# Unread products on TensorE: ahead of the first loads, in the attention's first batch, and between the gate's logits

## The chip, the cores and the metric

The kernel runs on one core of a Trainium2 chip. Its engines are TensorE (PE; its weight loads are shown apart as PEld), VectorE (DVE), ScalarE (ACT), GpSimd (POOL) and SyncE (SP), whose queue issues the DMAs. Each runs its own queue in order and waits for the others on semaphores. The metric is the device time of one execution in microseconds (us), as the median of several runs. [...]

## The reference

Attention over 2 batches, 8 heads, 576 positions and 64 dimensions, once on positions averaged in fours and once in a band of width 4, summed; then 8 dense experts that a Sinkhorn iteration weighs; then one MLP with softplus.

```python
    q_d = q.reshape(B, H, Sd, factor, D).mean(axis=3)        # k_d, v_d alike
    out_up = np.repeat(sm_attn(q_d, k_d, v_d), factor, axis=2)
    mask = np.abs(pos[:, None] - pos[None, :]) < factor
    scores = np.where(mask, scale * np.matmul(q, k.transpose(0, 1, 3, 2)), -1000000000.0)
    ...
    x = (out_up + out_local).transpose(0, 2, 1, 3).reshape(B * S, H * D)     # 1152 x 512

    logits = x @ w_gate                                       # 512 x 8
    P = np.exp(logits - logits.max())
    for _ in range(8):
        P /= P.sum(1, keepdims=True) + 1e-09
        P /= P.sum(0, keepdims=True) + 1e-09
        P *= N / E
    for e in range(E):
        out += P[:, e:e + 1] * (np.maximum(x @ w1[e], 0.0) @ w2[e])

    h = out @ w_in                                            # 512 x 2048
    return (np.maximum(h, 0.0) + np.log1p(np.exp(-np.abs(h)))) @ w_out
```

## The kernel before

The attention works in eight units, four of the first batch and then four of the second; a unit is two heads. A unit has four blocks: `c`, the coarse scores of all 144 averaged positions, and 0, 1, 2, the band in three thirds. `load` (L492) fetches a unit's q and k (`qk`, one buffer only, so that the next unit's load can begin only when the last transposes of this one have read it) and its values in two forms (`vw`, `vd`). `setup(g)` (L514, g = 0, 1, 2) transposes a third of q and k on PE (tile `tb`, L523); VectorE and ScalarE make `kT`, `fine`, `flat` and `qkd` of it. `scores` (L551) multiplies them into a PSUM bank `sc`: L557 for the coarse block, L564 (mask) and L570 for a third of the band. VectorE and ScalarE do the softmax and leave the weights in `ex`. `turn` (L588) transposes `ex` (tile `tp`, L596 coarse, L605 band), ScalarE copies it to `et`, and `values` (L609) multiplies it by the values (tile `pv`, L616 coarse, L627 band). In the first batch the banks of `sc` rotate over three (`m0` to `m2`), those of `tb` and `tp` over four (`at`), and `pv` has one (`y`).

The main loop (L1028) walks through the stream of 32 blocks with `turn` two and `values` three blocks behind `scores`, and sets a unit's `setup` beside the last two blocks of the one before. Beside the first batch it fetches the first expert's weights (`fetch_first`, `fetch_second`: a load to `raw`, casts on ScalarE to `w1h` and `w2h`, remainders and sums on GpSimd). The vectors x, and the sums and differences of them that a seven-product scheme needs, are split into two parts, `xh` and `xl` (`operands`, L419). From the second batch on, `beside` (L987) mixes in the first expert's products, `m` (L831) and `yps` (L919).

After the attention the second half of the operands is made, and `gates` (L672) computes the logits: `lt` (L683), a product with 16 columns of `wgs`, is copied to `lts` by ScalarE, and nine small products `lg` (L690; each with 16 rows, 128 columns of `lts` as weights and 8 columns of `fold`) write the logits of 128 positions each into one bank, of which only the first 72 columns are read. Two rounds of `m` products follow (`lead`).

Up to here the order of the instructions on each engine is set when the program is built, by a scheduler that runs a model of the engines and puts each instruction where it becomes ready; it may move an instruction ahead of others on its engine as long as the data allow it. From the loop after that on (L1098), the order is written out by a planner with fixed durations.

## Time and profile before

| | us |
|---|---|
| median of 3 runs | 1078.72 (1078.42 to 1078.95) |
| profiled execution, its own time | 1076.35 |
| its span, first to last instruction | 1074.3 |
| PE busy in the span | 1047.9 (98%) |
| DVE, ACT, POOL busy | 698.1, 568.5, 556.9 |
| longest in the chain that ended last | `yps` L919 40%, `m` L831 36% |

The profile is one execution, read by the hardware profiler; times in its rows are us from the span's start. Busy time of PE counts an instruction as long as it is in the pipe, so neighbours overlap: what a product costs in a stream is the distance between starts.

### The profile page before, as it was taken

How to read it: one execution, taken by the hardware profiler on the slowest of the kernel's cores; microseconds unless marked ns; L12 is line 12 of the kernel's file. 1: busy time of each engine (PE TensorE's matmuls, PEld its weight loads, DVE VectorE, ACT ScalarE, POOL GpSimd, SP SyncE). 2: the span in 40 equal slices, each digit the busy share in tenths (PEclk: the TensorE clock that was granted, in tenths of full speed). 3: DMA queues.
4: the chain of work that ended last, by engine and by line, in shares of the span. 5: the costliest groups of instructions: out<-in, count | busy, mean ns of one | idle time of the engine just before them, and what ended most of it. 6: DMA issues, size and time to landing. Idle time of an engine off the chain costs nothing.

```text
span 1074.3 us, 17657 instructions
## 1 busy us (share of the span) xinstructions
PE 1047.9 (98%) x6385; PEld 932.8 (87%) x6385; DVE 698.1 (65%) x1430; ACT 568.5 (53%) x1475; POOL 556.9 (52%) x575
## 2 busy tenths in 40 slices
PE   6989999999999999999999999999999999999998
PEld 5768888888989999898999989898988999789987
DVE  4797655776566566665656566565664778776765
ACT  4788634444444444454444444444454667676663
POOL 4567514477575565555556566664575412232221
PEclk9899989999999999999999999999999999999999
DMA  7553301122433334333333333343334473253112
GB/s 169 115 141 86 92 1 40 60 87 86 145 97 94 113 93 133 98 118 118 114 117 93 94 102 105 105 117 118 118 98 138 145 294 140 108 228 136 69 40 89
DMA packets 133495, 119.69 MB, mean 111 GB/s; under 512 B 35744, under 2 KB 111776, under 8 KB 133408
## 3 DMA queue, kind: packets, MB, share of 16 engines
q1 hardware_dynamic: 133408, 118.56, 35.6%
q8 instruction: 50, 0.82, 0.3%
q14 instruction: 37, 0.30, 0.1%
HBM read 93.11 MB, written 25.43 MB: 110 GB/s over the span
## 4 chain that ended last, share of the span: by engine, by line
PE 82%; DVE 9%; ACT 4%; POOL 1%; issue 1%; SPq 1%; DMA 1%; ACTq 0%
PE yps L919 40%; PE m L831 36%; DVE ab L798 1%; POOL ab L795 1%; DVE ab L791 1%; ACT one L793 1%; PE sc L570 1%; DVE xl L441 1%; DVE one L789 1%; PE tb L523 1%; PE tp L605 1%; DMA qk<-in_k 1%; PE pv L627 1%; SPq L499 1%; DVE c L850 1%
## 5 line engine op out<-in xcount | busy, mean ns | idle before, releaser
L831 PE MATMUL m<-xh,w1h 128*128 128x320 f32 (+1 forms) x1120 | 334.2, 299 | 3.6 <-DVE hl L770 1.6
L831 PE MATMUL m<-xh,w1l 128*128 128x320 f32 (+1 forms) x1120 | 332.8, 297 | 0.0
L831 PE MATMUL m<-xl,w1h 128*128 128x320 f32 (+1 forms) x1120 | 332.6, 297 | 0.0
L831 PEld LDWEIGHTS m<-xh,w1h 128*128 128x128 f32 x1120 | 212.6, 190 | 21.1 <-ACT t L843 3.5
L831 PEld LDWEIGHTS m<-xl,w1h 128*128 128x128 f32 x1120 | 212.7, 190 | 13.0 <-DVE xl L441 0.2
L831 PEld LDWEIGHTS m<-xh,w1l 128*128 128x128 f32 x1120 | 212.5, 190 | 0.3 <-issue 0.2
L919 PE MATMUL yps<-w2h,hh 128*128 128x512 f32 x502 | 198.9, 396 | 2.2 <-ACT hh L800 2.2
L919 PE MATMUL yps<-w2l,hh 128*128 128x512 f32 x502 | 198.2, 395 | 0.0
L919 PE MATMUL yps<-w2h,hl 128*128 128x512 f32 x502 | 196.0, 390 | 0.0
L919 PE MATMUL yps<-w2h,h 128*128 128x512 f32 x436 | 153.0, 392 | 0.1
L850 DVE TENSOR_TENSOR c<-m,t 128x256 f32<-128x256 f32 (+1 forms) x160 | 72.8, 455 | 113.8 <-PE m L831 67.5
L295 POOL TENSOR_TENSOR w1l<-sums,w1h 128x512 fp32r<-128x512 f32 x72 | 99.6, 1395 | 86.9 <-ACT w1h L293 75.3
L316 POOL TENSOR_TENSOR w2l<-raw,w2h 128x512 fp32r<-128x512 f32 x72 | 98.7, 1390 | 59.6 <-ACT w2h L314 56.1
L795 POOL TENSOR_TENSOR ab<-one,ab 128x320 f32<-128x320 f32 (+1 forms) x64 | 54.6, 855 | 143.6 <-ACT one L793 143.6
L768 ACT ACTIVATE hh<-c 128x256 fp32r<-128x256 f32 (+1 forms) x138 | 60.7, 445 | 128.5 <-DVE c L850 128.5
L949 DVE SCALAR_TENSOR_TENSOR acc<-yps,pr,acc 128x512 f32<-128x512 f32 x117 | 87.3, 746 | 55.2 <-PE yps L919 54.5
L770 DVE SCALAR_TENSOR_TENSOR hl<-c,hh 128x256 fp32r<-128x256 f32 (+1 forms) x138 | 94.7, 690 | 32.1 <-ACT hh L768 30.4
L919 PEld LDWEIGHTS yps<-w2h,hl 128*128 128x128 f32 x502 | 94.4, 188 | 21.7 <-DVE hl L802 0.2
L919 PEld LDWEIGHTS yps<-w2h,hh 128*128 128x128 f32 x502 | 94.7, 189 | 15.2 <-ACT hh L800 2.6
L843 ACT COPY t<-m 128x256 f32<-128x256 f32 (+1 forms) x160 | 63.4, 398 | 79.6 <-PE m L831 79.3
L919 PEld LDWEIGHTS yps<-w2l,hh 128*128 128x128 f32 x502 | 94.7, 189 | 10.9
L919 PEld LDWEIGHTS yps<-w2h,h 128*128 128x128 f32 x436 | 82.0, 188 | 15.2 <-ACT h L800 0.3
(136 smaller groups left out, 1653.6 us busy)
## 6 DMA issues: line engine op xcount, KB each, us to landing
raw<-in_moe_w SPq DMA_DIRECT2D x72, 256.0 KB
raw<-in_moe_w SPq DMA_DIRECT2D x36, 512.0 KB
w1h<-s_in SPq DMA_DIRECT2D x10, 896.0 KB
w1l<-s_in SPq DMA_DIRECT2D x10, 896.0 KB
raw<-in_moe_w_in SPq DMA_DIRECT2D x32, 256.0 KB
raw<-in_moe_w_out SPq DMA_DIRECT2D x16, 512.0 KB
w2l<-s_out SPq DMA_DIRECT2D x10, 512.0 KB
w2h<-s_out SPq DMA_DIRECT2D x10, 512.0 KB
```

The lines of the kernel that those rows point to most:

```text
L295: behind(chain, nc.gpsimd.tensor_tensor(lo[:, part], sums, hi[:, part].bitcast(F32), op=ALU.subtract))
L316: behind(chain, nc.gpsimd.tensor_tensor(lo[:, i], raw[:, i], hi[:, i].bitcast(F32), op=ALU.subtract))
L441: nc.vector.tensor_tensor(xl[s][:, i, kk], src, xh[s][:, i, kk].bitcast(F32), op=ALU.subtract)
L499: nc.sync.dma_start(qk[w * QT : (w + 1) * QT, cut, hh], src[b, h0 + hh].rearrange("(t p) d -> p t d", p=QT)[:, cut],)
L768: nc.scalar.activation(hh, c, AF.Relu)
L770: nc.vector.scalar_tensor_tensor(out=hl, in0=c, scalar=0.0, in1=hh.bitcast(F32), op0=ALU.max, op1=ALU.subtract)
L795: nc.gpsimd.tensor_tensor(ab, one, ab, op=ALU.subtract)
L831: nc.tensor.matmul(b[:, :h], x[:, i, kk, :], y[s][:, i, kk, :], start=(not more and n == 0), stop=(n == 5), skip_group_check=more,)
L843: nc.scalar.copy(t, b[:, :h])
L850: nc.vector.tensor_tensor(c, b[:, :h], t, op=ALU.add)
L919: nc.tensor.matmul(y, a[:, f, tok], b[:, f, :], start=(start and m == 0), stop=(stop and m == 5))
L949: nc.vector.scalar_tensor_tensor(out=acc[t], in0=y, scalar=pr[:, t, e : e + 1], in1=acc[t], op0=ALU.mult, op1=ALU.add,)
```

## The change

A helper `stir` puts unread products of the bf16 identity with itself, four times side by side (512 columns), into a bank that is overwritten afterwards. Eight stand ahead of the first `setup`. In unit 0 one stands ahead of the scores of each of the four blocks, two ahead of the coarse transposes and one ahead of each band block's; in units 1 to 3 one ahead of the coarse transposes and one ahead of each band block's. That makes 29. In `gates` an unread product of 256 columns, of `xh` with itself, follows every second logit product, four in all; it writes columns of the bank that nobody reads.

```diff
+    def stir(out, times):
+        for _ in range(times):
+            nc.tensor.matmul(
+                out.rearrange("p (a c) -> p a c", c=P), identb, identb.unsqueeze(1).to_broadcast([P, 4, P]),
+                start=True, stop=True,
+            )
...
         def __init__(self, n, b, u):
-            self.b, self.u = b, u
+            self.n, self.b, self.u = n, b, u
...
             sc = self.bank("sc", 0)
+            stir(sc, 1 if self.n == 0 else 0)
             if blk == "c":
...
                     tp = self.bank("tp", 1)
+                    stir(tp, 1 if self.n == 0 or self.n < 4 and c == 0 else 0)
                     for i in range(NB):
...
                 tp = self.bank("tp", 1)
+                stir(tp, 1 if self.n < 4 else 0)
                 for i in range(NB):
...
                 nc.tensor.matmul(lg[:, t * E : (t + 1) * E], lts[:, o : o + P], fold, start=True, stop=True)
+                if t % 2:
+                    busy = xh[s][:, 4, 0]
+                    nc.tensor.matmul(lg[:, 2 * P : 4 * P], busy[:, :P], busy[:, : 2 * P], start=True, stop=True)
...
     stream = [(x, blk) for x in units for blk in blocks]
+    stir(units[0].bank("pv", 2), 8)
     for g in range(NB):
         units[0].setup(g)
```

The scheduler sets the order up to the planner's loop anew. On PE, at the third unit's transposes of q and k (`tb`) and the second unit's coarse transposes (`tp`), where pass 2 of the prediction begins, there stood:

```order
L570 MATMUL sc<-kT,fine_150 128x72 x3
L523 MATMUL tb<-ident,qk 128x128 x6
L627 MATMUL pv<-et,vw 64x64 x12
L596 MATMUL tp<-ident,ex 72x96 x6
L564 LDWEIGHTS identb
L564 MATMUL sc<-mask,identb 128x216
L570 MATMUL sc<-kT,fine_151 128x72 x3
```

and now stands:

```order
L578 MATMUL sc<-kT,fine_150 128x72 x3
L637 MATMUL pv<-et,vw 64x64 x6
L530 MATMUL tb<-ident,qk 128x128 x6
L481 LDWEIGHTS identb
L481 MATMUL tp<-identb 128x512
L637 MATMUL pv<-et,vw 64x64 x6
L605 MATMUL tp<-ident,ex 72x96 x6
L572 LDWEIGHTS identb
L572 MATMUL sc<-mask,identb 128x216
L578 MATMUL sc<-kT,fine_151 128x72 x3
```

One unread product has come between, and half of the value products has moved ahead of the transposes of q and k.

On PE at the logits (`lg`), between products of the next round (`m`), there stood:

```order
L831 MATMUL m_2155<-xh_2027,w1l 128x320
L690 MATMUL lg<-fold,lts 128x8 x6
L831 MATMUL m_2127<-xh_2027,w1h 128x320
L831 MATMUL m_2127<-xl_2028,w1h 128x320
L831 MATMUL m_2127<-xh_2027,w1l 128x320
```

and now stands:

```order
L844 MATMUL m_2189<-xh_2057,w1l 128x320
L700 MATMUL lg<-fold,lts 128x8 x2
L703 MATMUL lg<-xh_103 128x256
L700 MATMUL lg<-fold,lts 128x8 x2
L703 MATMUL lg<-xh_103 128x256
L700 MATMUL lg<-fold,lts 128x8 x2
L703 MATMUL lg<-xh_2057 128x256
L844 MATMUL m_2161<-xh_2057,w1h 128x320
```

The unread products stand after each pair of logit products. The last three logit products, six `m` products further on before, now come after three `m` products, with the fourth unread product among them.

On SP, where the second unit's loads are issued (its `vw` first at the ends and then in the middle, its `qk`, its `vd`), there stood:

```order
L505 DMA vw<-in_v 72x2x64 x2
L499 DMA qk<-in_q 64x9x64 x2
L499 DMA qk<-in_k 64x9x64 x2
L509 DMA vw<-in_v 72x7x64 x2
L512 DMA vd<-in_v 72x2x256 x2
```

and now stands:

```order
L512 DMA vw<-in_v 72x2x64 x2
L516 DMA vw<-in_v 72x7x64 x2
L506 DMA qk<-in_q 64x9x64 x2
L506 DMA qk<-in_k 64x9x64 x2
L519 DMA vd<-in_v 72x2x256 x2
```

The larger part of `vw` has moved ahead of `qk`.

## Rows read from the trace of the kernel before

**Rows 1.** The page: granted TensorE clock in 40 slices of the span, in tenths.

```profile
PEclk9899989999999999999999999999999999999999
```

**Rows 2.** Stretches: width, busy us (instructions) of PE, PEld, DVE, ACT, POOL; PEclk; DMA.

```profile
12.00:30.00 18.00, 15.44 (x81) 12.45 (x81) 8.35 (x28) 8.97 (x42) 6.24 (x11) 1.00 0.73 169
30.00:42.00 12.00, 9.96 (x114) 8.11 (x112) 9.75 (x34) 10.26 (x51) 1.64 (x4) 1.00 0.49 103
42.00:54.00 12.00, 11.58 (x67) 9.55 (x67) 8.71 (x31) 9.58 (x38) 11.25 (x13) 0.57 0.69 147
54.00:70.00 16.00, 11.96 (x135) 9.83 (x134) 15.68 (x42) 12.20 (x47) 12.33 (x14) 1.00 0.54 144
...
80.00:140.00 60.00, 60.00 (x523) 51.42 (x523) 39.30 (x111) 39.91 (x148) 35.13 (x37) 1.00 0.32 82
...
152.00:160.00 8.00, 8.00 (x34) 7.65 (x35) 2.21 (x7) 1.78 (x6) 0.00 (x0) 0.57 0.01 2
```

**Rows 3.** Timeline of PE, first units: start, duration, operation, idle time before and its releaser.

```profile
6.72 2.15 PE L523 MATMUL tb<-ident,qk 128*128 128x128 f32 x9 [6.72 <-DMA vd<-in_v]
...
14.55 1.54 PE L523 MATMUL tb<-ident,qk 128*128 128x128 f32 x6 [0.65 <-DMA qk<-in_k]
18.00 1.15 PE L596 MATMUL tp<-ident,ex 96*72 96x96 f32 x6 [1.91 <-DVE ex L585]
...
24.57 1.43 PE L570 MATMUL sc<-kT,fine 128*128 128x72 f32 x6
...
29.86 0.82 PE L523 MATMUL tb<-ident,qk 128*128 128x128 f32 x6
```

**Rows 4.** Timeline of PE, the next pass.

```profile
32.64 0.69 PE L596 MATMUL tp<-ident,ex 96*72 96x96 f32 x6 [0.25 <-DVE ex L585]
...
33.90 0.49 PE L523 MATMUL tb<-ident,qk 128*128 128x128 f32 x3
...
38.70 0.80 PE L570 MATMUL sc<-kT,fine 128*128 128x72 f32 x6
40.18 0.85 PE L523 MATMUL tb<-ident,qk 128*128 128x128 f32 x6 [0.68 <-DMA qk<-in_k]
```

**Rows 5.** Timeline of PE, the pass after that, and the fifth unit's first transposes.

```profile
42.99 1.17 PE L596 MATMUL tp<-ident,ex 96*72 96x96 f32 x6 [0.25 <-DVE ex L585]
...
44.14 1.43 PE L570 MATMUL sc<-kT,fine 128*128 128x72 f32 x6
...
53.16 0.86 PE L570 MATMUL sc<-kT,fine 128*128 128x72 f32 x6
...
54.45 0.88 PE L523 MATMUL tb<-ident,qk 128*128 128x128 f32 x6
```

**Rows 6.** Timeline of VectorE: the identity in bf16.

```profile
1.74 0.21 DVE L459 CAST identb<-ident 128x128 bf16<-128x128 f32 x1
```

**Rows 7.** The chain that ended last: start, us on the chain, what.

```profile
36.44 3.61 DMA qk<-in_k
...
101.08 2.76 PE yps L919 x12
...
181.83 1.75 PE m L831 x12
```

**Rows 8.** Timeline of PE, the logits and the products after them.

```profile
150.41 1.50 PE L690 MATMUL lg<-fold,lts 16*128 16x8 f32 x12 [0.47 <-ACT lts L687]
...
153.40 1.45 PE L690 MATMUL lg<-fold,lts 16*128 16x8 f32 x6
...
158.15 0.47 PE L831 MATMUL m<-xh,w1h 128*128 128x320 f32 x1
158.41 0.47 PE L831 MATMUL m<-xl,w1h 128*128 128x320 f32 x1
```

**Rows 9.** Waits of PE from 140 to 200 us: us in total, times, longest.

```profile
PE m L831 <- DVE hl L770: 1.6, 2, 1.1
```

**Rows 10.** Timeline of VectorE behind the logits.

```profile
158.38 0.49 DVE L850 TENSOR_TENSOR c<-m,t 128x320 f32<-128x320 f32 x1 [2.73 <-PE m L831]
```

## The prediction

> **What bounds the kernel now.** I read the slices of the page first: the granted clock of TensorE is below 9 tenths in two places of the span's first sixth and nowhere after it [rows 1]. So only the first 160 us can be worth anything here. The stretches of those 160 us come next [rows 2]. From 80 to 140 us PE is busy 60.00 of 60.00 us at clock 1.00: there a time saved earlier is simply passed on, because nothing but PE's own queue sets the pace. From 42 to 54 us the clock is 0.57, from 152 to 160 us 0.57 again. [...]
>
> The column reads 1.00 from 12 to 30 us as well, but the operations say otherwise. Six score passes (L570) take 1.43 us at 24.57 [rows 3] but 0.80 us at 38.70 [rows 4], and 1.43 us again at 44.14, where the clock is granted at half [rows 5]. So PE ran at half from its first product at 6.72 until about 29.5, and the column is empty there rather than right.
>
> One unit of the attention is thus seen three times. I call a pass what PE does from the first transposes of one unit's coarse weights (L596) to the first transposes of the next-but-one unit's q and k (L523). Pass 1 goes from 18.00 to 29.86, 11.9 us, almost all at half [rows 3]. Pass 2 goes from 32.64 to 39.50 (38.70 + 0.80), 6.9 us, at full [rows 4]. Pass 3 goes from 42.99 to 54.02 (53.16 + 0.86), 11.0 us, most at half [rows 5]. In pass 1 no idle time stands before the rows after 18.00: PE was occupied and yet slow. Its work there is transposes and narrow products. [...]
>
> **The change, part by part.** (1) *Before the first loads.* Eight products on the bank `pv`, and three of the four on `sc`, stand ahead of the first transposes on PE. The identity is ready at 1.95 (1.74 + 0.21) [rows 6], the first transposes wait for the load until 6.72 [rows 3]. A product of 512 columns takes 0.23 us at full (12 in 2.76) [rows 7], so 0.46 at half. Eleven take 2.5 to 5.1 us and end between 4.5 and 7.0. The load hides them; the worst case costs 0.3. I take 0.
>
> (2) *Up to 18.00.* Unit 1's transposes still wait for its load (14.55, after DMA qk) [rows 3]; SP now issues the second unit's `vw` ahead of its `qk`, while it waited for the first unit's transposes anyway, so I count that as nothing, up to 0.5 us late. At full these six transposes take 0.85 as at 40.18 [rows 4], not 1.54, and VectorE's chain behind them starts that much sooner. Gain 0 to 0.8, I take 0.5. PE idles here for 1.91 us before 18.00 [rows 3], so the clock may fall again.
>
> (3) *Pass 1.* Full against half is 11.9 - 6.9 = 5.0 us. Four unread products stand in it: 4 x 0.23 = 0.9. If the clock holds throughout, the gain is 4.1; if it stays at half as before, the pass is 4 x 0.46 = 1.8 us longer. I take 3.1, a release about two microseconds into the pass, since the wait ahead of it is the emptiest place in the batch.
>
> (4) *Pass 2* was at full. It gets 0.9 us of products, and the wait of 0.68 for unit 3's q and k [rows 4] shrinks. That load starts when the third group of transposes (33.90 + 0.49) frees its only buffer, and lands 5.7 us later, most of it transfer (3.61) [rows 7]. One product (0.23) stands ahead of that group, so the load lands 0.2 later and PE comes 0.9 later. Cost 0.25.
>
> (5) *Pass 3.* Full against half is 11.0 - 6.3 = 4.7 us (6.9 less the 0.57 of value products that lie beyond it here), less 0.9 for four products: 3.8. But here ScalarE is busy 9.58 and GpSimd 11.25 of 12 us, with the casts of the first experts' weights [rows 2]. ScalarE was filled to 10.26/12 = 0.86 at best in 30 to 42 us; at that share 9.58 us of work need 11.2 us, and the gain would be 0.8. I take 2.0, nearer the ScalarE end, since only part of those casts stand on the attention's way.
>
> (6) *54 to 80 us.* VectorE is busy 15.68 of 16 us up to 70 [rows 2]: it sets the pace, its work is unchanged, so it neither adds to the gain nor eats it, if it was given its work earlier. From 20 to 54 us it has room for that: in 42 to 54 it idles 3.3 us, and a gain of 5 leaves it about as full as in 30 to 42 (9.75 of 12). The builder also interleaves the MoE products in another order; PE idles 4 us of it up to 70, so that can move 1 us either way. I take 0.
>
> Sum up to the gate: 0.5 + 3.1 - 0.25 + 2.0 = 5.3 us, between -5 and +8.5.
>
> (7) *The gate.* Twelve logit passes take 1.50 us at full, six take 1.45 at half [rows 8]. Each has 16 rows and 8 columns: PE is occupied and does next to nothing, and right after the first twelve the clock falls, with 0.47 us of waiting ahead of them and no other idle time. [...] The MoE products behind them start 0.26 to 0.27 us apart (158.15, 158.41) [rows 8] instead of 0.146 (12 in 1.75) [rows 7], a factor of 1.8. So 6.9 us at half hold 3.1 us that full speed gives back. The four added products of 256 columns cost at least 0.12 each (0.146 x 256/320) and at most a pair of logit passes, 0.25; I take 0.2, since each brings its own weights between unlike neighbours: 0.8. Gain 2.3. If the clock falls nevertheless they cost at half up to 4 x 0.5 = 2, and I take 0.8. What follows is late for PE: PE waits twice for VectorE's `hl`, 1.6 us in all, between 140 and 200 us [rows 9]; but VectorE waited for PE before (2.73 us before `c` at 158.38) [rows 10], so its chain moves up with PE and the gain is kept.
>
> **How the numbers follow.** 5.3 + 2.3 = 7.6 us. The span goes from 1074.3 to 1066.7, the profiled execution from 1076.35 to 1068.75. That one execution is 2.37 us below the median of the three runs (1078.72); I take the same 7.6 from the median: **1071.1 us**. About 0.2% (2.2 us) is what a measurement of this kernel can tell from no change.
>
> **The rivals.**
> *A, the gate keeps its fall.* The logits still hold PE at next to nothing for over 1.5 us, and four short products may be too few. What speaks for it is that the fall came though full-speed products ran until the logits began. Then 5.3 - 0.8 = 4.5: 1074.2. [...]
> *B, the other engines keep the time.* Pass 3 is paced by ScalarE and GpSimd, the gain of pass 1 is spent waiting for VectorE between 54 and 80 us [rows 2]; 2 us are left there, with the gate 4.3: 1074.4. Against it: VectorE's idle time before 54.
> *C, the products do not hold the clock in the first batch*, so that the change does not do what it says there: it rises for the loads, falls in the waits before 18.00 and in pass 3 as before, and the half microsecond of (2) and part of pass 1 just pay for the products. The gate's 2.3 alone minus about 1: 1077.4.
> *D, slower.* The products run, and the clock stays at half in passes 1 and 3 and at the gate. Then 1.8 + 1.8 + 0.25 in the passes and 0.8 to 2 at the gate are lost: about 5 us, 1083.7. It decides as soon as pass 1 gains less than its 1.8 us of products and the gate falls as well. For it: PE was slow while occupied; against it: between 54 and 70 us the clock stays at 1.00 with PE busy only 11.96 of 16 us [rows 2], as soon as the first MoE products run among the same attention work.
>
> **Chances.** Forecast 0.45, A 0.20, B 0.15, C 0.10, D 0.10. Faster by over 0.2% holds the forecast, A and B: 0.80; within 0.2% C: 0.10; slower D: 0.10. The range leaves out D and the best tail: its top is C with 1 us to spare, 1078.5; its bottom the sum with the upper ends of (2), (3), (5) and a gate at 3 us less the 0.25 of (4), 11.5 us, with 1 to 2 us from the new order: 1065.5.
>
> **What would show it.** Right: at 24 us of the new trace six score passes take 0.80, not 1.43; the first transposes of the fifth unit's q and k come 5 us sooner than 54.4; the granted clock is 1.00 from 30 to 60 and through the gate; the logits' neighbours start 0.146 apart. Wrong: a stretch at 0.50 in either place; a PE wait on ScalarE's `et` or VectorE's `ex` that grows in pass 3; equal times of the MoE products at 80 us. The forecast fails most easily at (5), where three engines are close to full, and at (7), where four short products must do.

## The result, and the profile after

The change made the kernel slower. Over six runs its median is 1083.80 us (1083.14 to 1088.29), where the kernel before had 1078.62 in the same session; the ratio is 1.0070, 95% interval [1.0049, 1.0091]. The forecast was 1071.1, and 1078.5 was the top of the range. The profiled execution took 1083.37 us with a span of 1081.3, 7.0 more than the span before.

The row of the granted clock on the page of the changed kernel, against [rows 1]:

```profile
PEclk8879999999999999999999999999999999999999
```

By this row it has become worse, not better; but the row of the kernel before reads too high in its first slice, since PE ran at half there until some 29 us (six score passes take 1.43 us at 24.57 [rows 3]) and the column is empty. The second slice is the same in both, the third has fallen from 9 to 7. Stretches of the changed kernel, with the columns of [rows 2]: width, then busy us and instructions of PE, PEld, DVE, ACT and POOL, then PEclk and DMA:

```profile
12.00:30.00 18.00, 15.44 (x120) 12.56 (x122) 10.29 (x34) 10.49 (x55) 5.46 (x11) 0.82 0.78 163
30.00:42.00 12.00, 9.39 (x111) 7.62 (x107) 9.99 (x37) 9.46 (x43) 3.13 (x6) 1.00 0.50 106
42.00:54.00 12.00, 11.63 (x58) 9.12 (x60) 6.53 (x20) 6.75 (x23) 9.26 (x11) 0.57 0.59 141
54.00:70.00 16.00, 13.04 (x120) 10.65 (x120) 14.11 (x35) 10.40 (x43) 10.10 (x13) 0.89 0.44 112
70.00:80.00 10.00, 7.74 (x51) 6.23 (x52) 8.94 (x31) 8.00 (x34) 6.36 (x6) 0.65 0.50 138
```

From 42 to 54 us the clock is 0.57 again, as in [rows 2], in spite of the products; from 54 to 70, where it was 1.00, it is 0.89, and 0.65 in the ten after that. In slices of 0.5 us the granted clock, a share of full speed, reads 1.00 or 0.50 and a value between only where it changes (here 0.85 at 42.0, 0.50 from 42.5 to 52.5, 0.91 there, 1.00 behind it). So a stretch's mean gives its time at half: 0.57 over 12 us is (1 - 0.57)/0.5 = 86% of them, 10.3 us. Beside that, PE waits at new places. The timeline of PE in the changed kernel (start, duration, operation, then in brackets the idle time before it and its releaser):

```profile
2.00 3.27 PE L481 MATMUL pv<-identb 128*128 128x512 bf16 x8 [2.00 <-DVE identb L459]
...
6.51 1.18 PE L530 MATMUL tb<-ident,qk 128*128 128x128 f32 x9 [0.59 <-DMA qk<-in_k]
...
11.90 2.83 PE L578 MATMUL sc<-kT,fine 128*128 128x72 f32 x12 [4.04 <-ACT fine L548]
...
20.04 0.69 PE L605 MATMUL tp<-ident,ex 96*72 96x96 f32 x6 [1.39 <-DVE ex L593]
...
20.88 0.80 PE L578 MATMUL sc<-kT,fine 128*128 128x72 f32 x6
...
28.78 0.85 PE L530 MATMUL tb<-ident,qk 128*128 128x128 f32 x6 [1.05 <-DMA qk<-in_k]
...
31.61 0.69 PE L605 MATMUL tp<-ident,ex 96*72 96x96 f32 x6 [1.27 <-DVE ex L593]
...
42.37 1.17 PE L605 MATMUL tp<-ident,ex 96*72 96x96 f32 x6 [1.59 <-DVE ex L593]
...
58.70 0.69 PE L605 MATMUL tp<-ident,ex 96*72 96x96 f32 x6 [1.72 <-DVE ex L593]
```

The eleven products ahead of the first transposes tell that the clock rose amid them: the seventh, at 4.5, takes 0.63 us and the eighth, at 4.9, 0.38. The transposes take 1.18 at 6.51, against 2.15 [rows 3]. Pass 1 then ran at full: six score passes take 0.80 at 20.88, against 1.43, and from its first transposes to those of the third unit's q and k it took 28.78 - 20.04 = 8.7 us in place of 11.9, the 3.1 us that the forecast wrote for it. But pass 1 began 2.0 us late (20.04 against 18.00), and every coarse turn now waits 1.3 to 1.7 us for `ex`, where in passes 2 and 3 it waited 0.25 [rows 4, 5], with another 0.65 in the middle of the value products ahead of it. At the start a wait of 4.04 us for `fine` is new, and VectorE's timeline of the changed kernel shows where it comes from:

```profile
10.07 0.61 DVE L677 TENSOR_TENSOR wg<-wg 128x16 f32<-128x16 f32 x1 [1.99 <-DMA wg<-in_moe_w_gate]
10.60 0.54 DVE L535 TENSOR_REDUCE qkd<-tb 128x96 f32<-128x384 f32 x1
11.07 0.60 DVE L547 COPY fine<-tb 64x192 f32<-64x192 f32 x2
```

The sum of the gate's weights, which PE uses only from 147 us on, stands in front of the copies `fine` and waits for its own load; in the kernel before it stood behind the second of them. It looks like the cause of the late pass 1. Experiments e4 and e18 show that there is another behind it.

Where the whole 7 us are lost is seen by setting the two kernels side by side at the same places. The first coarse turn comes 2.0 us late, the third 0.6 us early (42.37 against 42.99 [rows 5]): by then pass 1 has made the late start good. The fourth, at 58.70 above, stood here in the kernel before, in PE's timeline:

```profile
55.16 0.41 PE L596 MATMUL tp<-ident,ex 96*72 96x96 f32 x3
```

So 4.2 us go between the third and the fourth turn, with 10.2 us at half clock there in both kernels. Four unread products stand among that work. The first logits come 6.6 us late (157.03 against 150.41 [rows 8]); between the fourth turn and them the changed kernel has 13.7 us at half and the kernel before none.

### The profile page after: what moved, and what is told of

Read it like the earlier page. It is cut to its first block, busy times and chain, and to the rows that moved or that the text cites. A ratio compares the mean times of both kernels' runs of the same rounds, so it can differ in the third digit from the quotient of the medians.

```text
span 1081.3 us, 17708 instructions
## 1 busy us (share of the span) xinstructions
PE 1055.4 (98%) x6418; PEld 936.3 (87%) x6418; DVE 701.9 (65%) x1430; ACT 567.3 (52%) x1475; POOL 556.0 (51%) x575
## 4 chain that ended last, share of the span: by engine, by line
PE 82%; DVE 9%; ACT 4%; POOL 1%; issue 1%; DMA 1%; SPq 1%; ACTq 0%; DVEq 0%
PE yps L932 40%; PE m L844 36%; DVE xl L441 2%; DVE ab L811 2%; PE sc L578 1%; POOL ab L808 1%; DVE ab L804 1%; ACT one L806 1%; DVE one L802 1%; PE tp L615 1%; PE pv L637 1%; PE pv L626 1%; ACT sc L590 1%; PE tp L605 1%; DVE hl L815 1%
```

## The experiments

Two causes offer themselves. *Order*: the scheduler deals the whole attention anew when products are added, and the new order is worse. *Products*: their own time on PE, or a clock that they do not hold. They can be told apart because the kernel can be built twice: the first build gives the order of every engine, the second carries it over by order edges that wait for nothing, with other products in it.

```diff
-    with tile.TileContext(nc, schedule_with_timeline_sim=True) as tc:
-        attention_moe_mlp(tc, *args)
+    nc, arrays, orders = build(FIRST)
+    nc, arrays, _ = build(SECOND, orders)
...
+        for a, b in zip(row, row[1:]):
+            edge(b, a)
```

FIRST and SECOND say which unread products stand in the build: none in FIRST gives the order of the kernel before, all in FIRST that of the changed kernel. Unread products change no value that is used. All ratios are to runs of the kernel before on the same chip, with 95% intervals; "clock" is the mean granted clock over the runs.

| run | order | unread products | median us | ratio | clock |
|---|---|---|---|---|---|
| before | before | none | 1077.3 (137 runs) | 1 | 0.989 |
| after | after | as changed | 1083.8 | 1.0070 [1.0049, 1.0091] | 0.982 |
| e1 | before | as changed | 1081.7 | 1.0051 [1.0028, 1.0074] | 0.982 |
| e2 | after | none | 1084.8 | 1.0078 [1.0061, 1.0095] | 0.984 |
| e3 | nearly before | gate, 4 | 1079.8 | 1.0021 [1.0008, 1.0034] | 0.987 |
| e4 | after, `wg` put back | as changed | 1083.5 | 1.0055 [1.0039, 1.0070] | 0.984 |
| e5 | before | start, 8 | 1078.6 | 1.0007 [0.9990, 1.0023] | 0.983 |
| e6 | before | units, 21 | 1078.0 | 1.0002 [0.9988, 1.0017] | 0.987 |
| e7 | before | in PE's waits | 1077.4 | 0.9991 [0.9977, 1.0006] | 0.989 |
| e9 | its own | start, 8 | 1083.1 | 1.0057 [1.0029, 1.0086] | 0.980 |
| e10 | its own | units, 21 | 1079.4 | 1.0014 [0.9996, 1.0032] | 0.990 |
| e11 | before | gate, 27 | 1081.9 | 1.0047 [1.0029, 1.0066] | 0.989 |
| e12 | before | units, 63 | 1075.2 | 0.9982 [0.9965, 0.9998] | 0.996 |
| e13 | after | units, 63 | 1079.7 | 1.0034 [1.0014, 1.0053] | 0.993 |
| e18 | after, `wg` and `vw` put back | as changed | 1079.8 | 1.0019 [1.0001, 1.0038] | 0.985 |
| e14 | before | start and units, 8 + 42 | 1075.6 | 0.9989 [0.9971, 1.0007] | 0.993 |
| e15 | before | start and units, 8 + 63 | 1075.5 | 0.9980 [0.9965, 0.9994] | 0.995 |
| e17 | before | in PE's waits, more | 1076.5 | 0.9982 [0.9962, 1.0002] | 0.992 |

The clock column needs care: as the prediction noted, PEclk reads 1.00 up to some 30 us where the products still tell half, as from 6.72 to about 29.5 in the kernel before. In the changed kernel the column agrees with the products from 6.5 us on: 1.00 where its first transposes take 1.18 at 6.51, and 0.50 where twelve score passes take 2.83 at 11.90. So the clocks of kernels whose first half clock the column shows look worse beside the others' than they are.

**e1, e2: order or products.** SECOND has all products in e1 and none in e2.

> All the unread products of the changed kernel, each straight ahead of the product it was written ahead of, but every other instruction of each engine in the order of the kernel before. Theory order (the 5 us lost come from the new order that the scheduler made, the products themselves give back what pass 1 and the gate gain): about 1078.6 - 3.1 (pass 1) - 1.2 (gate) = 1074.3 us, 1072 to 1077; no 4-us wait of PE at 8 to 12 us, the first turn of coarse scores at about 18.0. Theory products (their own time, or a clock that stays at half, is what costs): 1082 to 1085 us, as the changed kernel.

> The order of the changed kernel on every engine, with none of its unread products. Theory order: the loss stays and the gains of the clock in pass 1 (3.1) and at the gate (1.2) go, so 1083.8 + 3 to 4 = about 1087 us, 1084 to 1089. Theory products: the time of the kernel before, 1078.6, within 1.5 us.

Neither theory had it alone. The order without a single product loses 0.78%, 8 us: as much as the whole change, within the intervals. But the products in before's order lose 0.51% as well. PE's timeline in e2 repeats the waits of the changed kernel:

```profile
36.33 1.18 PE L673 MATMUL tp<-ident,ex 96*72 96x96 f32 x6 [1.27 <-DVE ex L661]
...
48.64 0.69 PE L673 MATMUL tp<-ident,ex 96*72 96x96 f32 x6 [1.92 <-DVE ex L661]
...
62.77 0.69 PE L673 MATMUL tp<-ident,ex 96*72 96x96 f32 x6 [1.72 <-DVE ex L661]
```

So these waits belong to the order. Half of a unit's value products stand ahead of the transposes of q and k now, as the order shown ahead of the prediction has it; in the kernel before they stood behind them and filled the time in which VectorE and ScalarE make `ex`. That time is now a wait. Whether it is a loss is another question, since the products have been done earlier; e13 and e18 answer it. Nor are e2's 8 us the price of the waits alone: its six score passes still take 1.43 us at 37.48, where those of the kernel before take 0.80 at 33.27, so that PE also ran at half for longer.

**e3, e5, e6: the parts, in before's order.** Only the gate's four products, only the start's eight, only the 21 in the units.

```diff
             sc = self.bank("sc", 0)
-            stir(sc, 1 if self.n == 0 else 0)
...
-    stir(units[0].bank("pv", 2), 8)
```

> Only the four unread products between the gate's logits; the order of the rest is nearly that of the kernel before. If the gate's products shorten the half clock as the trace of the changed kernel reads (sinkhorn's first transpose 5.4 us late where everything ahead was 6.6 late): 1078.6 - 1.2 = 1077.4 us, and the half-clock stretch after 158 us about 3.3 us in place of 6.75. If they only add their own time: 1078.6 to 1079.3.

> Only the eight unread products ahead of the first transposes, everything else in the order of the kernel before. Theory conserved (the half-clock time of the attention is not removed by the products but comes back at the next wait of PE, here the 1.8 us ahead of 14.1 or of 17.0): the first twelve score passes take 1.7 us instead of 2.83, the first turn of coarse scores comes at 17.0 instead of 18.0, after that half clock as before; 1076 to 1079 us, 0 to 1 us below the kernel before. Theory released (once released the clock holds while PE has work): pass 1 at full, 4 to 5 us below the kernel before.

> Only the 21 unread products in the units, everything else in the order of the kernel before. Theory conserved: 18 of them stand on PE's path between 17 and 56 us, at 0.23 to 0.42 us each, 4 to 6 us, and the half-clock time stays; part of it is given back where PE waits for VectorE at 55 to 80 us: 2 to 5 us above the kernel before. Theory released: pass 1 and pass 3 at full, 2 to 5 us below the kernel before. Theory order (the loss of the changed kernel is the scheduler's order alone): at or below the kernel before.

Start and units change nothing that can be measured; the gate costs 0.2%. In the profile of e5 the start's eight products bought nothing at all: the first transposes behind them take 2.15 us, as in [rows 3]. In e6 the clock fell at 17.4 us, behind PE's wait of 1.81 for `ex`, and stayed at half to 27.6, in pass 1, with its four products in it, although PE did not idle there. The timeline of PE in e6:

```profile
19.39 1.43 PE L646 MATMUL sc<-kT,fine 128*128 128x72 f32 x6
...
29.21 0.80 PE L646 MATMUL sc<-kT,fine 128*128 128x72 f32 x6
```

One product in each place did not raise the clock there. Nor did the products in pass 1 raise it in the changed kernel: there the clock rose at 18.5 us, ahead of pass 1, after 6.8 us at half in which PE ran from 11.90 to 18.65 with hardly any idle time. Whether the products in pass 1 then held it no run shows.

**e8, e16: the same programs in a second execution.** Open was whether the half-clock places belong to the program.

> The kernel before once more, for a second profile of the same program. If the places of half clock are set by the program: the same as in the first profile, 43 to 53.3 us and 152 to 158.7 us, and none at 917 us. If they differ from execution to execution: other places or lengths, in steps of 3.4 us, and the time moves by about 0.45 us for each us at half.

> The changed kernel once more, for a second profile. If its half-clock places belong to its order: again at 42, 59, 73 and 162 us. If they differ from execution to execution as those of the kernel before: other places, in steps of 3.4 us; the waits of PE for VectorE's coarse weights of 1.4 to 1.9 us per unit stay, as they belong to the order.

They do not. Two stretches of the kernel before in its second execution, of 1078.34 us:

```profile
54.00:70.00 16.00, 14.20 (x107) 11.90 (x103) 15.63 (x41) 11.63 (x45) 12.39 (x15) 0.65 0.53 144
70.00:80.00 10.00, 10.00 (x67) 9.29 (x67) 6.83 (x22) 6.84 (x27) 3.79 (x4) 0.53 0.35 92
...
152.00:160.00 8.00, 7.53 (x47) 6.84 (x46) 3.59 (x10) 3.05 (x9) 0.00 (x0) 0.87 0.01 2
```

In the profile on which the forecast rested, 54 to 70 us read 1.00 and the gate 0.57 [rows 2]; here it is the other way round. Counted in slices of 1 us, and without the first 30 us that the column does not show, the first execution was at half for 10.2 us from 43 and 6.7 from 152, the second for 6.7 from 45, 20.4 from 59 and 3.3 from 158. The changed kernel in its second execution (1079.79) was at half for 6.8 us from 11, 3.4 from 32, 6.8 from 45, and 3.4 us each from 59, 76 and 158; in its first 6.8 from 11, 10.2 from 42, 3.4 from 59, 10.2 from 73 and 3.2 from 162. PE's wait of 3.8 us for `fine` and its waits for the coarse `ex`, 5.8 us in four, were there both times (4.0 and 6.0 in the first), so they do belong to the order. The places of half clock moved between two executions of one program, in both pairs of profiles, and the prediction had priced each place from one execution.

**e4: the gate's weights put back.** The three instructions of `wg` stand on VectorE and ScalarE where the kernel before has them; all else is the changed kernel.

```diff
+    dve[5:13] = [dve[n] for n in (6, 7, 8, 5, 10, 11, 12, 9)]
+    act[3:7] = [act[n] for n in (4, 5, 6, 3)]
```

> The changed kernel with three instructions put back: the sum of the gate's weights, its rounding and its remainder stand on VectorE and ScalarE behind the first fine copies, as in the kernel before. Theory order: PE's wait of 4.0 us at 8 to 12 us and the 2.0 us by which the first turn came late go, so about 1083.8 - 2.0 = 1081.8 us (1081 to 1082.5); the later losses stay. If the clock also holds through the start, half of another us. Theory products: no change, 1083.8.

The medians differ by 0.3 us, and the ratios by 0.15% with intervals that overlap: not the 2 us expected. PE's timeline in e4 shows the next wait behind the one removed:

```profile
9.46 1.56 PE L646 MATMUL sc<-kT,fine 128*128 128x72 f32 x12 [1.44 <-ACT fine L616]
...
16.80 1.51 PE L598 MATMUL tb<-ident,qk 128*128 128x128 f32 x6 [4.47 <-DMA qk<-in_k]
...
19.88 1.17 PE L673 MATMUL tp<-ident,ex 96*72 96x96 f32 x6 [0.71 <-DVE ex L661]
```

Unit 1's q and k land 2.2 us later than in [rows 3] (14.55), and the first turn still comes at 19.88. SP's timeline of the changed kernel (start and duration of an issue) says why:

```profile
7.90 0.90 SPq L516 DMA_DIRECT2D vw<-in_v  x2
8.92 1.29 SPq L506 DMA_DIRECT2D qk<-in_q  x2
```

SP issues q and k when it did before (8.90), since they wait for their buffer anyway. But the larger part of `vw`, issued a microsecond ahead of them and not behind them as before, now stands in front of them in the DMA engines: from 9.5 to 10.5 us, in halves, these move 192 and 200 GB/s, where in the kernel before they moved 14 and 79. In every profile with this order on SP the transposes come at 16.3 to 16.9 (both of the changed kernel, e2, e4, e13), and in every one with `qk` first at 14.1 to 14.9, whatever products there are (both of before, e1, e3, e5 to e7, e9 to e12, e14, e15, e17).

**e18: the values put back too.** e4, and on SP that part of `vw` behind `qk`.

```diff
+    sp[13:19] = [sp[n] for n in (15, 16, 17, 18, 13, 14)]
```

> The changed kernel with the gate's weights put back as in e4, and on SP the larger part of the second unit's vw issued behind its q and k as in the kernel before. Theory transfer (the vw ahead in the DMA engines is what delays the load): the first transposes of unit 1 at 14.1 to 14.7 us, not 16.8, the first coarse turn at 17 to 18, and about 2 us less than e4: 1081.5, 1080.5 to 1082.5. Theory other (the load is late for another reason, or the 2 us are taken back later): transposes at 16.3 to 16.9, or 1083 to 1084 in spite of an earlier start. The waits of the later coarse turns, 1.3 to 1.7 us each, stay in both.

Two issues moved on SP's queue, and most of the loss is gone: 1.0019 against 1.0055 in e4, 0.36% or 3.9 us, with intervals that just fail to overlap; taken together they leave 1.3 to 6.5 us. PE's timeline in e18:

```profile
14.69 1.54 PE L598 MATMUL tb<-ident,qk 128*128 128x128 f32 x6 [1.34 <-DMA qk<-in_k]
...
17.79 1.17 PE L673 MATMUL tp<-ident,ex 96*72 96x96 f32 x6 [0.71 <-DVE ex L661]
...
43.09 0.69 PE L673 MATMUL tp<-ident,ex 96*72 96x96 f32 x6 [1.53 <-DVE ex L661]
```

The load lands as before, and the first turn comes at 17.79. The waits of the later coarse turns are still there, and the third turn comes at 43.09, against 42.99 in the kernel before; what they cost by themselves e13 shows. By the ratios more was won than the 2.1 us at the first turn. The two profiles do not show the rest on the way: the first logits come 1.4 us sooner than in e4 (154.39 against 155.83), and behind them e4 has a fall of the clock at 925 us, worth about 1.5, that e18 has not. In the second execution of the changed kernel, with nothing put back, they came at 154.41. So the late load is shown at the first turn, and how much of it reaches the end is not.

**e7, e17: products only where PE waits.** Before's order, and no products inside the passes but in the first unit's scores.

```diff
+            stir(tb, (0, 6, 2, 2)[self.n] if g == 0 and self.n < 4 else 0)
...
-                    stir(tp, 1 if self.n == 0 or self.n < 4 and c == 0 else 0)
+                    stir(tp, (7, 3, 3, 3)[self.n] if c == 0 and self.n < 4 else 0)
```

> Before's order, with unread products of 512 columns only where PE waited anyway in the kernel before: eight ahead of the first transposes, one ahead of each block's scores of unit 0, six ahead of unit 1's first transposes, seven ahead of each coarse turn of unit 0, and two or three in the same places of units 1 to 3. Theory waits (the clock falls because PE has a wait, and holds where the wait is filled with products): no half clock between 6 and 43 us, pass 1 gains 4 to 5 us, 1073 to 1075. Theory conserved: the half-clock time comes back within pass 1 or behind it, 1077 to 1081.

> Before's order, unread products only where PE waits: eight ahead of the first transposes, one ahead of each block's scores of unit 0, six, ten and six ahead of the first transposes of units 1, 2 and 3, seven ahead of each coarse turn's first half in unit 0 and five in units 1 to 3. Theory waits: the 2.1 us of waiting at 25 us are filled, the clock holds from 8 to 56 us, and without products inside the passes the time is below three in every place: 1071 to 1074. Theory spread (the clock asks for products all along the pass): half clock again inside pass 2 or 3, 1075 to 1079.

In e7 pass 1 ran at full, from 17.35, and what it gained met a transfer. PE's timeline in e7:

```profile
17.35 0.69 PE L674 MATMUL tp<-ident,ex 96*72 96x96 f32 x6 [0.51 <-DVE ex L662]
...
23.62 0.80 PE L647 MATMUL sc<-kT,fine 128*128 128x72 f32 x6
...
26.96 0.85 PE L599 MATMUL tb<-ident,qk 128*128 128x128 f32 x6 [2.10 <-DMA qk<-in_k]
...
32.28 1.43 PE L647 MATMUL sc<-kT,fine 128*128 128x72 f32 x6
```

The third unit's transposes came 2.9 us earlier than in [rows 3], after a wait of 2.10 us for q and k, and the clock fell there and stayed at half for 17 us, all through pass 2 (0.94 from 12 to 30 us, 0.50 to 42, 0.87 to 54). With that wait filled as well (e17: six, ten and six products ahead of `tb`, seven and five ahead of the coarse turn) the clock was 1.00 from 12 to 54 us. It then fell at 58 and 71 us and at the gate in the profiled execution, for 6.8, 3.4 and 6.8 us; the time is 0.2% below before, at the edge of what can be told.

**e9, e10: the same parts with an order of their own.** Start alone and units alone, as the scheduler orders them, each moved in some 200 places on PE.

> Only the eight unread products ahead of the first transposes, and this time the order that the scheduler makes of it, which differs from before's in some 180 places on PE. In before's order the same products changed nothing (1.0007). Theory order (what a small edit does here is mostly that the scheduler deals the attention's order anew): a different time from that, by 3 us or more either way. Theory products: the same as with before's order, within 1.5 us of 1077.4.

> Only the 21 unread products in the units, with the order that the scheduler makes of them, which differs from before's in some 200 places on PE. In before's order the same products changed nothing (1.0002). Theory order: a different time from that, by 3 us or more either way. Theory products: within 1.5 us of 1077.4.

The start's eight products, worth nothing in before's order (1.0007), cost 0.57% with the scheduler's. The units' products cost no more with their own order than the measurement can tell. The order is thus a draw of its own at every edit: of the three drawn here two lose 6 to 8 us and one nothing that can be measured. In e9's own order unit 1's load is in time (14.59), so its loss has another cause. A subtraction of 4.03 us on VectorE, of the kind in the last section, stands in its profile, and 20 us at half clock between 52 and 79 us; neither is shown to be the cause.

**e11: the gate, 27 products.** Three behind each logit product.

```diff
-                if t % 2:
+                for _ in range(3):
...
```

> Before's order, none of the products but those at the gate, and there three unread products of 256 columns behind each of the nine logit products in place of one behind every second: 27 x 0.12 = 3.2 us of PE time against 0.5. Theory held (enough products keep the clock through the gate): no half clock between 150 and 165 us, which in the kernel before is 3.3 to 6.7 us, worth 1.5 to 3 us; so 0 to 2 us above the kernel before, and the products pay for at best themselves. Theory not held: half clock there as before, 3.2 to 4.5 us above the kernel before.

The clock was not held. Around the gate in e11:

```profile
152.00:168.00 16.00, 16.00 (x65) 14.38 (x65) 2.43 (x7) 1.79 (x6) 0.00 (x0) 0.57 0.00 0
```

PE is busy 16.00 of 16 us, yet at half for 13.6 us, six of them under `m` products of full width. In all the profiles together the gate's half-clock time is 0 to 6.9 us without products there and 3.2 to 6.8 with the four (both of the changed kernel, e1, e3, e4, e18), so nothing here shows that products at the gate help; what would is open.

**e12 to e15: more products in the units, and the order once more.** Two or three in each of the 21 places; e13 has after's order, e14 and e15 the start's eight too.

```diff
-                stir(tp, 1 if self.n < 4 else 0)
+                stir(tp, 3 if self.n < 4 else 0)
```

The other two places in a unit were changed alike.

> Before's order, and the 21 places in the units with three unread products each instead of one. Each product more costs 0.22 us at full clock where PE sets the pace. Theory dose (the clock holds in the units if enough products stand there): no half clock between 17 and 70 us, where the single products had 10.2 + 10.2 us; 42 x 0.22 = 9 us more work against 9 us given back, near the kernel before. Theory no hold: half clock as before, 6 to 12 us above the kernel before.

> The order of the changed kernel on every engine, with three unread products at each of the 21 places in the units, none ahead of the first transposes and none at the gate. Theory two causes (the order costs its own 5 to 8 us, whatever the clock does): the clock is held between 17 and 56 us, and the time is 1081 to 1085, 5 us or more above the same products in before's order (1075.2). Theory clock only (the order of the changed kernel costs because it lets the clock fall more often): 1074 to 1077, as in before's order.

> Before's order, two unread products at each of the 21 places in the units and the eight ahead of the first transposes. Theory dose: between one each (1078.0, half clock 10.2 us in pass 1 and 10.2 us at 58 us) and three each (1075.2, none): if two are enough, 21 x 0.22 = 4.6 us of PE time less than with three, of which a part lies beside other waits: 1071 to 1074 us. If two are too few: 1076 to 1080, with half clock of 3.4 to 10 us in a pass.

> Before's order, three unread products at each of the 21 places and the eight ahead of the first transposes. If the clock of the first transposes is worth anything beside the load that PE waits for at 14.5 us: 0.5 to 1 us below three each without them, 1074 to 1075. If the load and VectorE's chain set the first turn alone: the same, 1075.2 within 1 us.

With three in each place the clock was held, at 1.00 from 12 to 70 us. Stretches of e12:

```profile
12.00:30.00 18.00, 14.93 (x132) 10.77 (x131) 10.29 (x35) 10.83 (x56) 6.12 (x11) 1.00 0.74 168
30.00:42.00 12.00, 11.36 (x116) 8.53 (x112) 8.44 (x30) 8.25 (x38) 3.35 (x5) 1.00 0.46 103
42.00:54.00 12.00, 11.85 (x99) 9.04 (x97) 9.20 (x30) 10.55 (x42) 11.61 (x13) 1.00 0.77 165
54.00:70.00 16.00, 12.37 (x116) 8.87 (x116) 14.87 (x43) 12.66 (x51) 12.38 (x15) 1.00 0.55 146
```

and PE's timeline there, where the score passes tell that the column is right this time:

```profile
19.73 0.80 PE L646 MATMUL sc<-kT,fine 128*128 128x72 f32 x6
...
52.45 0.41 PE L673 MATMUL tp<-ident,ex 96*72 96x96 f32 x3
```

e12 and e15 beat the kernel before by intervals that just leave out 1; e7, e14 and e17 lie below it too, but with 1 inside. It is about 2 us, since 40 and more products cost 0.22 us each on PE (three take 0.65 in a stream), as far as no wait takes them up. The mean clock over twelve runs, 0.996 and 0.995, agrees that it was held. Two in each place come out the same as three within the intervals. With after's order the same 63 products hold the clock through the passes too (1.00 from 12 to 70 us in e13), and so show what the order costs by itself. PE's timelines, first of e12, whose fourth turn is the row at 52.45 above, then of e13:

```profile
17.81 0.44 PE L673 MATMUL tp<-ident,ex 96*72 96x96 f32 x3 [1.75 <-DVE ex L661]
...
42.51 0.66 PE L673 MATMUL tp<-ident,ex 96*72 96x96 f32 x6
```

```profile
16.70 0.85 PE L595 MATMUL tb<-ident,qk 128*128 128x128 f32 x6 [1.61 <-DMA qk<-in_k]
...
19.25 0.44 PE L670 MATMUL tp<-ident,ex 96*72 96x96 f32 x3 [1.05 <-DVE ex L658]
...
44.05 0.69 PE L670 MATMUL tp<-ident,ex 96*72 96x96 f32 x6 [0.79 <-DVE ex L658]
...
57.82 0.69 PE L670 MATMUL tp<-ident,ex 96*72 96x96 f32 x6 [1.07 <-DVE ex L658]
```

Here too unit 1's load lands at 16.70, and although both are at full clock up to 70 us, the fourth coarse turn comes 5.4 us later than in e12. Of that, 1.4 us are there at the first turn, behind the late load, and 1.5 at the third: in between the waits for `ex` cost nothing. Nearly 4 us come between the third and the fourth. There the coarse scores of the turn stand one band block later on PE (50.35 in e13, 46.27 in e12), and 24 more value products stand ahead of it, so part of the 4 us is work done sooner; but at the first logits e13 is still 5.5 us behind (154.62 against 149.10). The six profiles with after's order on PE (both of the changed kernel, e2, e4, e13, e18) take 13.8 to 16.3 us from the third turn to the fourth, and the twelve with before's order 9.8 to 12.2, whatever their products and their clock. By the ratios, 1.0034 against 0.9982, the order costs 0.5%, 5.6 us, with the same products; a part of that may be the clock again, which falls in e13's profile at 73 and 158 us (0.66 from 70 to 80 us, 0.88 from 152 to 160; mean over the runs 0.993, against 0.996).

## Why the prediction was wrong

**Step (2) failed.** The row was there, ahead of the prediction: SP issues the larger part of `vw` ahead of `qk`. The step saw that SP had time for it while it waited, and counted nothing, at most 0.5. SP did have the time; the DMA engines did not (192 and 200 GB/s from 9.5 to 10.5 us, against 14 and 79). Unit 1's transposes came 1.8 to 2.4 us late, and putting the two issues back brought the first turn 2.1 us forward and won 3.9 us by the ratios (1.3 to 6.5; e18 against e4). The gain of 0.5 that the step took from faster transposes did not come either: in the changed kernel they took 1.51 us at 16.34, not 0.85.

**Steps (5) and (6) failed at the order.** Step (5) wrote a gain of 2.0 us in pass 3 and asked nothing about the order there; step (6) allowed 1 us either way for the new order, behind 54 us, and took 0. From the third to the fourth coarse turn the changed kernel loses 4.2 us on the kernel before, with as much time at half clock and four unread products more; with full clock and equal products in both the order makes nearly 4 (e13 against e12), part of it work done sooner. The order as a whole costs 8 us without products (e2) and 5.6 with 63 in both (e13 against e12), each with some more half-clock time in it. The waits of 1.3 to 1.9 us at the coarse turns, which no step asked about, cost nothing up to the third. So the rows on PE that stood ahead of the prediction did what they read like, cost little, and drew the eye from the row on SP and from pass 3, of which no row was shown.

**Steps (3) and (5) had the dose wrong.** That one unread product in each place would raise the clock in the passes and keep it there was the author's assumption; no row of the kernel before shows it. Full speed in pass 1 was worth the 3.1 us written for it, and with three in each place the clock was 1.00 through all three passes (e12, e13). But with one in each place it was not: in e6 pass 1 ran at half (0.72 from 12 to 30 us), in the changed kernel pass 3 did (0.57 from 42 to 54). Here it took two or three, and then their own time eats most of what they give: about 2 us net (0.18 and 0.20% in e12 and e15), where 5.1 was written for (3) and (5) together.

**Step (7) failed in its sign.** The gate was priced at 2.3 us gained from a fall of 6.9 us seen in one execution. That length was the mean of 0.57 over 8 us, read as a share at half; slice by slice the fall was 6.7 us long. In the second execution of the same program it was 3.3 us long, and in e7, e12 and e14, without products there, it did not come. That four products would carry the clock through the logits was the author's estimate; they did not keep the fall away in any of the six profiles that have them, and they cost 0.2% (e3), about 2.3 us. Their own price was mis-sized too: in the changed kernel a pair of logit products and one unread product come 0.85 us apart, where two logit products took 0.50 [rows 8], so 0.35 each and not 0.2. PE's timeline of the changed kernel:

```profile
157.03 0.61 PE L700 MATMUL lg<-fold,lts 16*128 16x8 f32 x4 [0.46 <-ACT lts L697]
...
157.88 0.61 PE L700 MATMUL lg<-fold,lts 16*128 16x8 f32 x4
```

That is 1.4 us; for the rest of the 2.3 no row accounts.

**Steps (1) and (4) were right.** The start's products cost nothing (e5). They also bought nothing by themselves. In pass 2 the changed kernel takes 7.6 us from the coarse turn to unit 3's transposes (31.61 to 39.22), the kernel before 7.5, and the wait for that load has shrunk from 0.68 to 0.13: a cost of 0.1 for the 0.25 written, with twelve value products more in it.

**The rivals.** The time came out at D's, 1083.7, by luck: the point from which D decides did not hold, as pass 1 did gain its 3 us in the changed kernel. Of A it came true that the gate kept its fall (3.2 us from 162), and of C the fall in pass 3. B named VectorE as the engine that PE would wait for between 54 and 80 us; PE did wait there (3.6 us, on `xf` and `ex`), but over half of the loss, 3.5 of 6.6 us, was made by the fourth turn, at 58.70. No rival was an order that loses time by itself or a transfer that comes late, and that is what the range missed.

**What stays open.** e1, the same products in before's order, loses 0.5%, while its parts start, units and gate lose 0.07, 0.02 and 0.21%, and e18 with nearly after's order 0.19%. Four of e1's eight runs lie at 1078.9 to 1080.0 and four at 1083.3 to 1087.4; the four slower ones have a mean granted clock of 0.978 to 0.981, the four faster ones 0.982 to 0.989, so more time at half goes with them. What brings it no profile here shows, and e1 can't be taken as the price of the products.

## What to carry to other kernels

Where a scheduler sets the order, an added instruction is two changes, itself and a new draw of the order around it: carry the old order over by edges and time both apart, of a transfer that has moved ahead of another ask when the other lands (here 1.8 to 2.4 us later), not whether the queue had time to issue it, and set the two kernels side by side at the same places, to see where the time goes. A clock that falls at other places or for other lengths from one execution to the next (the gate's fall was 6.7 us long in one of the kernel before and 3.3 in the other) has to be read from several, since one profile gives the length that a fall had once and not its mean. Unread products held it here at two or three in a place and not at one (1.00 from 12 to 54 us in e14 and e12; 0.72 from 12 to 30 in e6), and their own time took back most of what that gave.

## What the runs showed of the hardware

One kind of subtraction took VectorE far longer in some executions than in others. In the changed kernel one subtraction of two SBUF operands, 0.41 to 1.02 us elsewhere between 59 and 83 us, took 3.74 us on VectorE, beside GpSimd operations that ran without a gap from 65.47 to 70.90. The timelines of VectorE and of GpSimd:

```profile
65.89 3.74 DVE L441 TENSOR_TENSOR xl<-xf,xh 128x256 fp32r<-128x256 f32 x1
```

```profile
65.47 0.73 POOL L244 TENSOR_TENSOR sums<-raw 128x256 f32<-128x256 f32 x1
66.16 1.27 POOL L316 TENSOR_TENSOR w2l<-raw,w2h 128x512 fp32r<-128x512 f32 x1
...
69.30 1.63 POOL L555 TENSOR_TENSOR vd<-vd 72x256 f32<-72x256 f32 x2
```

It ended at 69.63, soon after GpSimd's work on the weights gave way to `vd` (69.30). A subtraction of the kind takes 3.74 us in the profiles of e2 and e13 too and 4.03 in e9, and in no other profile. In the second execution of the changed kernel the same GpSimd operations ran beside it without a gap from 65.32 on, and it took 0.60 (at 65.73): the program does not settle whether it takes long. That GpSimd holds it up is the author's guess, which no run shows. What it costs was not measured by itself: e4's profiled execution took as long as the changed kernel's (1083.55 and 1083.37) with a subtraction of 0.60 in that place.

TensorE's clock fell while PE was occupied. In e11 it fell at about 154 us, amid logit passes and the products between them, with no idle time but 0.47 us ahead of them, and it stayed at half through 4.5 us of `m` products without a gap, from 162.89 to 167.43. And the same wait may or may not be followed by a fall: PE waits 2.15 us for `hh` at about 920 us in the profiles of both kernels, and the clock fell behind it in the first execution of the changed kernel and not in its second, nor in the two of before. Where it falls there, as in e3 at 919.4, 1.5 us are lost: thirty PE instructions later 8.5 us have gone, against 7.0 without it.
